# Splitting the first expert's weights on ScalarE and VectorE, with more list and expert steps for each attention tile

## The chip, the cores and the metric

The kernel runs on one core of a Trainium2 chip. The metric is the device time of the core in microseconds (us). Three runs of the kernel before took 971.29, 972.48 and 968.57 us; the median is 971.29 us. TensorE (PE) does the matmuls, VectorE (DVE) and ScalarE (ACT) the elementwise work, GpSimd (POOL) some elementwise work and the indirect DMAs, and SyncE (SP) issues most of the plain DMAs. Each engine works through its own list of instructions in order.

## The reference

Linear attention without a mask feeds a mixture of experts in which each token goes to two of eight experts:

```python
kv  = einsum('bhsd,bhse->bhde', k, v)            # 8 x 8 heads, 576 tokens, 64
out = einsum('bhsd,bhde->bhse', q, kv)
x   = out / sqrt(mean(out*out, -1) + 1e-6) * g_norm      # to [4608, 512]
noisy = x @ w_gate + log1p(exp(x @ w_noise)) * noise     # 8 experts
top2, weights = the two largest, softmax over them
y[t] = sum over the two experts e of weight * relu(x[t] @ w1[e]) @ w2[e]   # w1 512x1024, w2 1024x512
```

All is float32. The kernel gets near float32 accuracy in the experts by splitting each operand into two float16 parts, a high and a low one, and adding three float16 products.

## The kernel before, in words

**Attention stage.** The 4608 tokens are 36 tiles of 128 (t0 to t35); each of the 8 batches has four and a half of them. The loop at the end of the function goes over batches b and, in each, over its five pieces of tiles: every batch has one half tile, so tiles 4, 13, 22 and 31 come in two calls. A call of `tile_mm` (L590) multiplies a piece of q with the batch's `kvw`, into the PSUM tile `big`, of which there are two. `keep_warm` (L124) then adds matmuls of zeros, the fillers: KW = 8 a call while t < KT, KV2 = 0 from there. `steps` is `prep(b + 1)`, which makes the next batch's `kvw`: products of k and v (L558), a copy on ScalarE (L563), a transpose (L568), a copy `kvT` (L571), the gate products (L577) and a last copy into `kvw` (L580). `advance(t)` evacuates a tile on ScalarE (L598), squares and sums a pair of tiles (`sq` on ScalarE L605, `ss` on VectorE L607), makes the norm (`Ln` and `Exp` on ScalarE L611 and L612, three small VectorE operations), scales the pair on GpSimd (`lg` L621, `x` L625) and writes it out to `xs` in DRAM. A tile's matmul waits for the evacuation of the tile two before it.

**Lists.** `side` holds generators that make the expert lists, one for each chunk of tiles; the chunks end at tiles 10, 18, 28 and 36. `pump()` takes one step of each. A yield's number is how many pumps go by before the next step. `gating` finds the top two experts and counts places with matmuls into `RM` (L176, L178); `onehots` builds three tables on VectorE (`oa` L304, `ot` L307, `ob` L310); PY pumps later `place` (L318) multiplies them on PE. GY is the wait before the counting matmuls. For expert 0, `moe_early` then finishes the list, gathers the rows and, as soon as expert 0's weights are loaded, transposes them (`xpose`, L385 to L389) and queues `l1` (L434) and `l2` (L478) for two tiles, a unit, in `early`. `fill_early` takes one step of that queue. Three units of expert 0 are such early ones.

**First weights.** `w0 = first_weights()` is the generator `weights(0, wts_a, G, SL)`, of which the loop takes two steps a tile. It loads w1 of expert 0, takes column maxima on VectorE (`mx`, L221), shares them by a matmul with `dg` (L228, L232), and splits w1 in four slices of 128x1024; then the same for w2, whose load goes into the same buffer `rw`. In `split`, with `lo is G`, ScalarE scales a slice in place (L250), casts it to the float16 high part (L251), and GpSimd subtracts the two (L248). All later experts take the other branch: ScalarE scales and casts in one operation (L255), VectorE makes the low part in one operation (L257, L259).

**After the attention stage** the early units' remaining steps are taken from `early` (with list steps of expert 1, `locate`, between them: `oa`, `ot`, `ob` on VectorE and `place`), and then the loop over all other units runs. Its first unit in which the PE program branches on a count (`tc.Switch` in `l1`, L460 and L434) is the last unit of expert 0, here called the first switch.

All instructions stand in the order in which the code is written (`manual_schedule`), so these generators set the order on every engine.

## Time and profile before

| | |
|---|---|
| runs | 971.29, 972.48, 968.57 us |
| the profiled execution | 977.14 us, its span 975.3 us |
| mean granted TensorE clock | 0.965 |
| PE busy | 916.5 us (94%) |
| VectorE, ScalarE, GpSimd busy | 445.7, 327.5, 387.5 us |
| DMA | 143.33 MB, mean 147 GB/s |
| first attention tile's matmuls, last one's | start 19.2 us, start 153.3 us |
| first switch on PE | 234.0 us |

The profile is of one execution, whose own time is 5.9 us over the median of the runs. A page of it gives busy time by engine; the view of windows gives it for stretches of time together with the granted clock; the timeline lists instructions in order with the idle time before each and what released it.

### The profile page before, as it was taken

The page shows a single profiled execution, that of the slowest core. Times are in us where ns is not written, and L with a number is a line of the kernel's source. Part 1 is how long each engine was busy: PE and PEld are TensorE (multiplying, and loading weights), DVE is VectorE, ACT ScalarE, POOL GpSimd, SP SyncE. Part 2 cuts the span into 40 slices and gives each one's busy share as a digit, 9 for nine tenths or more (in the row PEclk, how much of TensorE's full clock was granted, in tenths as well). Part 3 has the DMA queues.
Part 4 walks back from the last instruction along what each step waited for, and adds up shares of the span by engine and source line. Part 5 has one row for each costly group of instructions (what it writes and reads, how often), then busy time and mean ns, then how long its engine had stood idle before and what let it go on. Part 6 is the DMA issues. An engine that isn't in the chain of part 4 may idle for free. (4 is left out here: it accounts for less than half of the span.)

```text
span 975.3 us, 15946 instructions
## 1 busy us (share of the span) xinstructions
PE 916.5 (94%) x6484; PEld 517.2 (53%) x6484; DVE 445.7 (46%) x936; ACT 327.5 (34%) x519; POOL 387.5 (40%) x412
## 2 busy tenths in 40 slices
PE   9976888988999999999999999999998989999995
PEld 8866775657444644464445444554443434644452
DVE  1648658554745543545353444455264447311110
ACT  1576543222522341233224332333243223332111
POOL 0456645153523542344245234414342544242122
PEclk9978799988999999999999999999999999999998
DMA  8999655952963864485357544666349735362224
GB/s 329 364 348 350 207 195 198 385 98 57 254 116 76 169 169 60 97 171 135 84 102 132 152 116 92 142 104 164 66 120 127 187 76 92 50 113 45 44 37 58
DMA packets 123534, 143.33 MB, mean 147 GB/s; under 512 B 79632, under 2 KB 79760, under 8 KB 123408
## 3 DMA queue, kind: packets, MB, share of 16 engines
q1 hardware_dynamic: 95696, 80.68, 30.2%
q0 software_dynamic: 17920, 41.95, 23.2%
q10 hardware_dynamic: 9792, 18.88, 5.1%
q8 instruction: 97, 1.59, 0.7%
q14 instruction: 29, 0.24, 0.1%
HBM read 83.02 MB, written 40.11 MB: 126 GB/s over the span
## 5 line engine op out<-in xcount | busy, mean ns | idle before, releaser
L434 PE MATMUL pp<-xT,w1h 128*128 128x512 f16 (+5 forms) x1600 | 367.8, 327 | 5.9 <-DVE oa L304 2.6
L478 PE MATMUL pp<-w2h,hT 128*128 128x512 f16 x1200 | 365.6, 381 | 5.4 <-ACT hT L439 4.1
L478 PEld LDWEIGHTS <-hT 128*128 128x128 f16 x1800 | 175.9, 98 | 214.0 <-issue 9.3
L412 POOL DMA_INDIRECT out_rows<-y,row x80 | 129.9, 1624 | 359.2 <-ACT y L503 354.5
L440 DVE SCALAR_TENSOR_TENSOR hT<-pp,hT 128x512 f16<-128x512 f32 x160 | 108.0, 688 | 353.7 <-ACT hT L439 353.6
L434 PE MATMUL pp<-xT,w1l 128*128 128x512 f16 (+5 forms) x800 | 256.8, 327 | 0.0
L478 PE MATMUL pp<-w2l,hT 128*128 128x512 f16 x600 | 228.2, 380 | 0.0
L434 PEld LDWEIGHTS <-w1h 128*128 128x128 f16 x1600 | 151.2, 100 | 112.2 <-issue 8.0
L439 ACT ACTIVATE hT<-pp 128x512 f16<-128x512 f32 x160 | 92.5, 596 | 265.7 <-PE pp L434 255.1
L503 ACT ACTIVATE y<-pp,gate 128x512 f32<-128x512 f32 x80 | 54.0, 686 | 258.6 <-PE pp L478 201.5
L360 POOL DMA_INDIRECT xg<-xs,idx x80 | 85.0, 1063 | 91.7 <-DVE la L332 43.5
L434 PEld LDWEIGHTS <-w1l 128*128 128x128 f16 x800 | 79.8, 100 | 56.5 <-issue 1.8
L368 POOL TENSOR_TENSOR xh<-xg,xh 128x512 f16<-128x512 f32 x70 | 91.4, 1380 | 35.7 <-ACT xh L367 35.6
L221 DVE TENSOR_REDUCE mx<-rw 128x1 f32<-128x1024 f32 x64 | 74.7, 1208 | 1.3 <-DMA rw<-w 1.3
L367 ACT ACTIVATE xh<-xg 128x512 f16<-128x512 f32 x70 | 41.1, 624 | 22.7 <-DMA xg<-xs,idx 18.8
L590 PE MATMUL big<-kvw,qt 64*128 64x80 f32 (+1 forms) x640 | 45.5, 287 | 2.2 <-ACT kvw L580 2.1
L304 DVE TENSOR_TENSOR oa<-jb,lnb 128x1152 bf16<-128x1152 bf16 (+2 forms) x32 | 46.3, 1448 | 0.0
L590 PEld LDWEIGHTS big<-kvw,qt 64*128 64x128 f32 (+1 forms) x640 | 39.1, 189 | 8.2 <-ACT kvw L580 2.8
L607 DVE TENSOR_REDUCE ss<-sq 128x16 f32<-128x1024 f32 x18 | 21.9, 1215 | 47.2 <-ACT sq L605 47.1
L411 POOL MEMSET tick<- 1x1 f32 x80 | 38.7, 484 | 0.0
L625 POOL TENSOR_TENSOR x<-o,ss 128x512 f32<-128x512 f32 x36 | 38.0, 1076 | 0.0
L257 DVE SCALAR_TENSOR_TENSOR w1l<-rw,sc,w1h 128x1024 f16<-128x1024 f32 x21 | 27.3, 1333 | 22.3 <-ACT w1h L255 22.3
(140 smaller groups left out, 587.7 us busy)
## 6 DMA issues: line engine op xcount, KB each, us to landing
rw<-w SPq DMA_DIRECT2D x64, 512.0 KB, 7.2
kvc<-kvm SPq DMA_DIRECT2D x32, 512.0 KB, 8.0
xs<-x ACTq DMA_DIRECT2D x18, 512.0 KB, 5.9
out_rows<-zrow ACTq DMA_DIRECT2D x18, 512.0 KB, 7.5
qt<-qt SPq DMA_DIRECT2D x8, 640.0 KB, 8.3
qt<-qt SPq DMA_DIRECT2D x8, 512.0 KB, 7.9
kvr<-kvr SPq DMA_DIRECT2D x4, 512.0 KB, 6.9
xg<-xs,idx POOLq DMA_INDIRECT x80, 3.9
```

Of the source, the lines that this page charges most:

```text
L221: V.tensor_reduce(mx[:, c:c + 1], src[:, c], axis=AX.X, op=OP.max, apply_absolute_value=True)
L304: V.tensor_tensor(oa, jb[:, None, :].to_broadcast([P, n, P]), lnb[:, s, e:e + 1].to_broadcast([P, n, P]), OP.is_equal)
L360: G.indirect_dma_start(out=x, out_offset=None, in_=src, in_offset=bass.IndirectOffsetOnAxis(ap=LI[e][:, t:t + 1], axis=0))
L367: A.activation(x[:, 0], XG[u, t], AF.Copy)
L368: G.tensor_tensor(x[:, 1], XG[u, t], x[:, 0], OP.subtract)
L412: d = G.indirect_dma_start(out=out, out_offset=bass.IndirectOffsetOnAxis(ap=LS[e][:, t:t + 1], axis=0), in_=y, in_offset=None, compute_op= ...
L434: T.matmul(ps[:, f % ps.shape[1], 0:n], w[wn][:, c, f * P:(f + 1) * P], x[:, xo + c, 0:n], start=(c == 0 and k == 0), stop=(c == HP - 1 an ...
L439: A.activation(h[:, 0, f:f + nf, 0:n], ps, AF.Relu)
L440: V.scalar_tensor_tensor(h[:, 1, f:f + nf, 0:n], ps, 0.0, h[:, 0, f:f + nf, 0:n], op0=OP.max, op1=OP.subtract)
L478: T.matmul(ps, h[:, hk, f, i * P:(i + 1) * P], w[wn][:, f], start=(f == 0 and k == 0), stop=(f == 7 and k == 2))
L503: A.activation(y, ps, AF.Copy, scale=LG[e][:, t:t + 1])
L590: T.matmul(TL[t][r0:r0 + n, h, hp * 80:(hp + 1) * 80], q[r, hp, s0 - o:s0 - o + n], KVW[b][r, hp], start=True, stop=True, skip_group_check ...
```

## The change

It has four parts.

1. The branch of `split` for GpSimd is gone. The first weights are split as all others: one ScalarE operation and one VectorE operation a slice. With the slack that only the first weights have, `split` yields after the ScalarE operation as well, so it takes ten steps where there were five; the up to three yields behind the first split are gone.
2. While t < EP = 24 the loop pumps the lists two more times a tile, so five times. GY goes from 3 to 5 and PY from 6 to 7.
3. `fill_early` is also called behind every call of `tile_mm`, so the early expert work advances by two steps a tile.
4. Fillers end at tile 14 where they ended at tile 24: 11 calls of 8 are gone, 88 matmuls of zeros.

```diff
-KT, KV2 = 24, 0
-XW, PY = 2, 6
+KT, KV2, EP = 14, 0, 24
+XW, PY = 2, 7
-GY = 3
+GY = 5
-    def weights(e, pool, lo, slack=0):
+    def weights(e, pool, slack=0):
-        def split(src, hi, lw, s):
-            if lo is G:
-                for c in range(5):
-                    if c:
-                        G.tensor_tensor(lw[:, c - 1], src[:, c - 1], hi[:, c - 1], OP.subtract)
-                    if c < 4:
-                        A.activation(src[:, c], src[:, c], AF.Copy, scale=s)
-                        A.activation(hi[:, c], src[:, c], AF.Copy)
-                    yield
-                return
+        def split(src, hi, lw, s, slack=0):
             for c in range(4):
                 A.activation(hi[:, c], src[:, c], AF.Copy, scale=s)
+                if slack:
+                    yield
                 if c:
-                    lo.scalar_tensor_tensor(lw[:, c - 1], src[:, c - 1], s, hi[:, c - 1], op0=OP.mult, op1=OP.subtract)
+                    V.scalar_tensor_tensor(lw[:, c - 1], src[:, c - 1], s, hi[:, c - 1], op0=OP.mult, op1=OP.subtract)
                 yield
-            lo.scalar_tensor_tensor(lw[:, 3], src[:, 3], s, hi[:, 3], op0=OP.mult, op1=OP.subtract)
+            V.scalar_tensor_tensor(lw[:, 3], src[:, 3], s, hi[:, 3], op0=OP.mult, op1=OP.subtract)
             yield
             yield
-        yield from split(r1, w["w1h"], w["w1l"], sc[:, 1:2])
-        for _ in range(min(slack, 3)):
-            yield
+        yield from split(r1, w["w1h"], w["w1l"], sc[:, 1:2], slack)
-        yield from split(r2, w["w2h"], w["w2l"], sc[:, 4:5])
+        yield from split(r2, w["w2h"], w["w2l"], sc[:, 4:5], slack)
         def first_weights():
-            yield from weights(0, wts_a, G, SL)
+            yield from weights(0, wts_a, SL)
...
                 tile_mm(*args)
+                fill_early()
                 keep_warm(KW if t < KT else KV2)
...
                 fill_early()
                 pump()
+                if t < EP:
+                    pump()
+                    pump()
...
-        yield from weights(e, wts_b if e % 2 else wts_a, V)
+        yield from weights(e, wts_b if e % 2 else wts_a)
```

What this moves is seen in the order of the instructions. First ScalarE behind the evacuation of tile 9 (`o<-big`), before; `rw<-rw,sc` and `w1h<-rw` are the two passes of the split, `kvw<-kvt` the copy that the next batch's transpose on PE needs:

```order
L598 ACTIVATE o<-big 128x640
L605 ACTIVATE sq<-o 128x1024
L250 ACTIVATE rw<-rw,sc 128x1024
L251 ACTIVATE w1h<-rw 128x1024
L250 ACTIVATE rw<-rw,sc 128x1024
L251 ACTIVATE w1h<-rw 128x1024
L563 ACTIVATE kvw<-kvt 128x4x64
L611 ACTIVATE ss<-ss,eps 128x16
L612 ACTIVATE ss<-ss 128x16
```

The same place now; the lines of the change's file are lower by 4 to 9:

```order
L589 ACTIVATE o<-big 128x640
L596 ACTIVATE sq<-o 128x1024
L246 ACTIVATE w1h<-rw,sc 128x1024
L554 ACTIVATE kvw<-kvt 128x4x64
L602 ACTIVATE ss<-ss,eps 128x16
L603 ACTIVATE ss<-ss 128x16
L589 ACTIVATE o<-big 128x640
L246 ACTIVATE w1h<-rw,sc 128x1024
```

Four passes of 128x1024 stood between `sq` and `kvw`; now it is one, and the next one stands behind the evacuation of tile 10.

Second, VectorE where the first chunk's tables are made, before (`vals` is the last step of the gating):

```order
L196 CAST vals<-gt_w 128x80
L304 TENSOR_TENSOR oa<-jb,lnb 128x1280
L307 TENSOR_TENSOR ot<-tb_101,t_115 128x100
L607 TENSOR_REDUCE ss<-sq 128x16
L310 TENSOR_TENSOR ob<-ot,vals 128x500
L630 TENSOR_REDUCE zl<-lg 128x32
```

And now:

```order
L196 CAST vals<-gt_w 128x80
L598 TENSOR_REDUCE ss<-sq 128x16
L295 TENSOR_TENSOR oa<-jb,lnb 128x1280
L221 TENSOR_REDUCE mx<-rw 128x1 x2
L298 TENSOR_TENSOR ot<-tb_101,t_115 128x100
L301 TENSOR_TENSOR ob<-ot,vals 128x500
L621 TENSOR_REDUCE zl<-lg 128x32
```

Two of w2's column maxima, which stood ahead of the gating's end, now stand between `oa` and `ob`. On PE the `place` that needs `ob` has moved from behind tile 19 to behind tile 17.

Third, VectorE just ahead of the first switch, before (`hT` is the low part of a unit's hidden layer):

```order
L440 SCALAR_TENSOR_TENSOR hT<-pp,hT 128x2x256
L307 TENSOR_TENSOR ot<-tb_101,t_115 128x90
L310 TENSOR_TENSOR ob<-ot,vals 128x450
L440 SCALAR_TENSOR_TENSOR hT<-pp,hT 128x2x256
L304 TENSOR_TENSOR oa<-jb,lnb 128x1152
L307 TENSOR_TENSOR ot<-tb_101,t_115 128x90
L310 TENSOR_TENSOR ob<-ot,vals 128x450
```

And now:

```order
L431 SCALAR_TENSOR_TENSOR hT<-pp,hT 128x2x256 x2
L295 TENSOR_TENSOR oa<-jb,lnb 128x1152
L298 TENSOR_TENSOR ot<-tb_101,t_115 128x90
L301 TENSOR_TENSOR ob<-ot,vals 128x450
L295 TENSOR_TENSOR oa<-jb,lnb 128x1152
L298 TENSOR_TENSOR ot<-tb_101,t_115 128x90
L301 TENSOR_TENSOR ob<-ot,vals 128x450
```

Behind the last `hT` there are two rounds of tables for expert 1's list where there was one; the `place` on PE that ends this stretch needs the last. From the first switch on PE's order is the same in both.

## The prediction

> **What bounds the kernel now.** I read the windows first: busy time by engine, then granted clock, DMA share and GB/s (columns PE, PEld, DVE, ACT, POOL).
>
> ```profile
> 44.00:51.70 7.70, 7.28 (x148) 6.35 (x146) 3.41 (x11) 5.40 (x8) 5.65 (x5) 1.00 0.89 328
> 51.70:68.00 16.30, 10.45 (x113) 8.70 (x114) 6.41 (x13) 12.61 (x21) 12.23 (x11) 0.59 0.89 328
> 68.00:88.90 20.90, 18.94 (x357) 17.04 (x354) 19.87 (x78) 8.42 (x18) 9.88 (x15) 0.99 0.96 371
> 88.90:109.00 20.10, 12.16 (x144) 10.37 (x144) 11.43 (x54) 14.81 (x24) 15.18 (x13) 0.58 0.63 221
> 109.00:155.00 46.00, 41.42 (x543) 33.12 (x543) 28.68 (x110) 23.81 (x48) 22.62 (x33) 0.96 0.56 190
> 155.00:234.00 79.00, 68.05 (x501) 47.54 (x500) 47.66 (x136) 21.50 (x35) 26.30 (x33) 0.92 0.67 207
> 310.00:950.00 640.00, 630.54 (x3459) 312.87 (x3457) 267.78 (x428) 198.33 (x297) 246.44 (x248) 0.99 0.54 109
> ```
>
> From 310 to 950 us PE is busy 630.54 of 640 us at full clock: nothing is to be had there, and the order is the same. What the change can move lies ahead of the first switch (234 us). There PE loses time in two ways. It stands idle: 5.85 us in 51.7 to 68, 7.94 in 88.9 to 109. And it runs slowly there: at 0.59, 10.45 busy us are 6.2 at full clock, a loss of 4.3; at 0.58, 12.16 lose 5.1. Those two windows lie on the two weight splits, and the view of waits for PE in 44 to 234 says on whom it waited (us, times, longest):
>
> ```profile
> PE kvt L568 <- ACT kvw L563: 5.9, 2, 3.9
> PE pp L385 <- DMA xg<-xs,idx: 5.9, 2, 3.6
> PE kvt L577 <- ACT kvT L571: 4.7, 2, 3.4
> PE M L318 <- DVE ob L310: 3.3, 1, 3.3
> ```
>
> The first and third are ScalarE's copies for the next batch, which queue behind the split. In the timeline, start and duration:
>
> ```profile
> 51.01 1.13 ACT L250 ACTIVATE rw<-rw,sc 128x1024 f32<-128x1024 f32 x1
> 52.18 1.06 ACT L251 ACTIVATE w1h<-rw 128x1024 f16<-128x1024 f32 x1
> ...
> 54.30 1.06 ACT L251 ACTIVATE w1h<-rw 128x1024 f16<-128x1024 f32 x1
> 55.27 0.36 ACT L563 ACTIVATE kvw<-kvt 128x256 f32<-128x256 f32 x1
> 55.69 1.06 PE L568 MATMUL kvt<-ident,kvw 128*64 128x128 f32 x4 [3.94 <-ACT kvw L563]
> ```
>
> Four passes from 51.01 on hold `kvw` to 55.27 and PE for 3.94 us; the clock then stays low to 68. So this stage is bound by a loop through PE, ScalarE and VectorE, each in order, and PE's clock punishes each wait. Between the splits, at 68 to 88.9, VectorE is the full engine: 19.87 of 20.9 us.
>
> **The change, part by part.** The new passes exist for expert 1 (mean ns behind the busy us; the VectorE row gives min/median/max), beside GpSimd's old one:
>
> ```profile
> L255 ACT ACTIVATE w1h<-rw,sc 128x1024 f16<-128x1024 f32 x8 | 8.9, 1136 | 0.0
> L257 DVE SCALAR_TENSOR_TENSOR w1l<-rw,sc,w1h x21: 1276/1283/2176, 193.2 to 817.4; 128x1024 f16<-128x1024 f32 x21
> L248 POOL TENSOR_TENSOR w1l<-rw,w1h x4: 2126/2127/2131, 49.5 to 58.9; 128x1024 f16<-128x1024 f32 x4
> ```
>
> For eight slices ScalarE gives up 8 x 1.06 = 8.5 us, GpSimd 8 x 2.13 = 17.0, and VectorE takes on 8 x 1.28 = 10.3. None of it is itself on PE; what counts is where PE's call of a tile lands. I line both kernels up by four calls: tiles 11, 14, 20, 23.
>
> ```profile
> 50.07 1.12 PE L590 MATMUL big<-kvw,qt 64*128 64x80 f32 x16
> ...
> 70.15 1.12 PE L590 MATMUL big<-kvw,qt 64*128 64x80 f32 x16
> ...
> 82.17 0.62 PE L124 MATMUL RM<-zrow 128*128 128x128 f16 x8
> 82.72 2.08 PE L558 MATMUL kvt<-kvc 128*64 128x64 f32 x64
> 84.74 0.68 PE L558 MATMUL kvt<-kvr 64*64 64x64 f32 x16
> 85.35 1.12 PE L590 MATMUL big<-kvw,qt 64*128 64x80 f32 x16
> ...
> 87.21 1.12 PE L590 MATMUL big<-kvw,qt 64*128 64x80 f32 x16
> ...
> 110.92 1.12 PE L590 MATMUL big<-kvw,qt 64*128 64x80 f32 x16
> ```
>
> From start to start, 8 fillers hold PE for 82.72 - 82.17 = 0.55 us and a batch's k-v products for 85.35 - 82.72 = 2.63.
>
> *Tiles 11 to 14* took 70.15 - 50.07 = 20.1 us, 5.8 of it idle and 4.3 low clock. `kvw` now stands behind one pass of 1.14 instead of four: its wait of 3.94 falls to about 0.5. The passes that went from ahead of it stand one each ahead of `kvT` and the batch's last copy; those copies also stand behind `Ln` and `Exp`, which wait for VectorE's `ss`. I put 1.8 us of wait at each. Idle is then 4.1 instead of 5.8, spread over three places, and I take the low clock as gone. Gain 1.7 + 4.3 = 6.0. Bounds: 1.7 if the clock falls all the same, 10.1 if no wait is left.
>
> *Tiles 14 to 20* took 17.1 us. Six calls' fillers go: 6 x 0.55 = 3.3 gained. Against it stands VectorE, whose rows here are
>
> ```profile
> 78.20 1.21 DVE L221 TENSOR_REDUCE mx<-rw 128x1 f32<-128x1024 f32 x1
> ...
> 82.35 1.48 DVE L304 TENSOR_TENSOR oa<-jb,lnb 128x1280 bf16<-128x1280 bf16 x1
> 83.75 0.40 DVE L307 TENSOR_TENSOR ot<-tb,t 128x100 bf16<-128x100 bf16 x1
> 84.07 1.21 DVE L607 TENSOR_REDUCE ss<-sq 128x16 f32<-128x1024 f32 x1
> 85.20 0.96 DVE L310 TENSOR_TENSOR ob<-ot,vals 128x500 bf16<-128x500 bf16 x1
> ```
>
> The `place` that needs `ob` now stands two tiles earlier on PE, and between `ss` and `ob` lie `oa` and two maxima of w2: from the end of tile 15's `sq` that is 1.2 + 1.5 + 2.4 + 0.4 + 1.0 = 6.5 us. PE has for this time two tile calls and the gate products, about 2.3 us: it waits some 4.2 us at `place`, and behind it are tile 18 and all else. The counting matmuls, a tile earlier too, wait about 1.7, and two more maxima ahead of tile 17's `ss` hold `Exp`, the evacuation behind it and tile 20 by about 1.4. So 7.3 us of new waits against 3.3: a loss of 4.0. Bounds: a gain of 3.3 if VectorE comes in time, a loss of 10 if the clock also falls to 0.58 over the stretch's 11.8 us of work (which would add up to 8.5, in part hidden under these waits).
>
> *Tiles 20 to 23* took 110.92 - 87.21 = 23.7 us: 7.9 idle, 5.1 low clock, four calls' fillers (2.2), the rest work. The second split's passes go one to a tile. I keep 2 us of wait at `kvT`. The batch's last copy now stands behind the second chunk's `Exp` for the gates, which waits for VectorE, and that for GpSimd's two gathers: I count 6.3 us of wait there, and 1.3 of low clock behind it. With two transposes (0.9) gone from here and 0.75 of counting matmuls come in, 23.7 becomes 17.4: gain 6.3. Bounds: 2.2 (fillers alone) to 13.
>
> *Tile 23 to the first switch.* Expert 0's second split ends later by tiles, so `l1` starts behind tile 28 instead of 24, but goes two steps a tile: by tile 35 its first unit's `l1` and `l2` are done, 30 matmuls further than before. The waits of this stretch I take as the same but for two:
>
> ```profile
> 170.44 0.97 PE L385 MATMUL pp<-ident,xg 128*128 128x128 f32 x4 [2.32 <-DMA xg<-xs,idx]
> ...
> 230.33 0.69 DVE L440 SCALAR_TENSOR_TENSOR hT<-pp,hT 128x512 f16<-128x512 f32 x1 [1.33 <-ACT hT L439]
> ...
> 232.48 0.63 DVE L310 TENSOR_TENSOR ob<-ot,vals 128x450 bf16<-128x450 bf16 x1
> 233.16 0.53 PE L318 MATMUL M<-ob,oa 128*128 128x50 bf16 x9 [3.27 <-DVE ob L310]
> ```
>
> The gathered rows of the third unit now have 96 matmuls ahead of their transpose where there were 60: the 2.32 us and some 1.5 of low clock behind it go, a gain of 3.8. Just ahead of the switch `ob` comes a round of tables later: between `hT`'s end (231.0) and `ob`'s (233.1) is 2.1 us, which PE waits in addition. Net gain 1.7; bounds -5 (every gather waits again) and +5.
>
> Sum: 6.0 - 4.0 + 6.3 + 1.7 = **10 us**. The profiled execution's span of 975.3 becomes 965.3; its own time, 977.14, lies 5.9 over the median of the runs, so from the median 971.3 I predict **961 us**.
>
> GpSimd loses 17 us of work that shared these stretches with VectorE, and this has a price of its own: a VectorE operation on two columns ended with the GpSimd pass beside it.
>
> ```profile
> 94.86 2.00 DVE L334 TENSOR_TENSOR row<-idx,la 128x2 int32<-128x2 int32 x1
> 94.72 2.13 POOL L248 TENSOR_TENSOR w2l<-rw,w2h 128x1024 f16<-128x1024 f32 x1 [1.95 <-ACT w2h L251]
> ```
>
> Both end at 96.86. The Trainium skill, "SBUF — State Buffer", section "SBUF: two separate sides", says that a VectorE operation with two SBUF inputs and a GpSimd operation that reads SBUF exclude each other for a whole instruction. The two rows agree. By this rule the new VectorE passes, which read `rw` and the high part, can each lose time to a GpSimd operation; the maximum of 2176 ns against a median of 1283 in the row above would be such a case. If half of eight lost 0.9, the second stretch would lose some 2 us more; I leave that inside its bounds.
>
> **The rivals.** *VectorE becomes the bound (chance 0.20).* The split, w2's maxima and the first chunk's tables fall on the engine that was 95% busy at 68 to 88.9. Then tiles 14 to 20 lose 10 and tiles 20 to 23 gain the fillers' 2.2 alone: 6.0 - 10 + 2.2 + 1.7 = 0, so 971. For it: the 19.87 of 20.9. Against: GpSimd's load is gone, and VectorE has gaps on both sides.
>
> *The clock stays low without fillers (chance 0.10, the slower side).* From tile 14 on PE has, by the windows, 18.9 + 7.1 + 39.8 = 65.6 us of work at full clock up to 155, less 6 of fillers: about 60, in the 86 us that I give it (tile 14 at 64, tile 35's end at about 150). At a clock of 0.58 that is 103: 17 more than the 86, so 10 - 17 = -7: 978. It decides from the point where the mean clock over this stretch falls under 60 / 96 = 0.63. For it: 0.59 and 0.58 where PE was busy for 64 and 60%, about the share that it will have from tile 14 to 23. Against: from tile 28 on `l1` fills PE, and at 90% busy the clock was 0.96.
>
> *Only long waits cost clock (chance 0.08).* A short wait did cost some:
>
> ```profile
> 133.00:140.00 7.00, 5.53 (x53) 4.32 (x51) 3.69 (x9) 3.53 (x10) 4.40 (x8) 0.76 0.47 170
> 135.87 0.63 PE L385 MATMUL pp<-ident,xg 128*128 128x128 f32 x4 [1.47 <-DVE ss L613]
> ```
>
> If this were rare, and a wait as short as the 1.7 and 2 us above left the clock at 1.0, the new stalls would overlap with work at full speed and the second stretch would lose 1 instead of 4: 958. The Trainium skill, "TensorE: Matmul & The Clock Gate", Part 1, says that the clock halves after an idle window of about 3.4 us. By that rule only the waits of 4.2 and 6.3 would cost; the row of 1.47 us speaks against it.
>
> **How the numbers follow.** My forecast has 0.62; it spans 954 to 967 by the terms' bounds, taken half way since not all go one way. Below 958 lies the third rival's side, above 967 the first and then the slower one. A range of 953 to 973 leaves out the slower rival and the far ends. A measurement tells a change of 0.5% (4.9 us) from none, so the marks are 966.4 and 976.2. Faster: nearly all of the forecast (0.58), the third rival (0.08) and a little of the first (0.04): 0.70. Same: 0.20. Slower: 0.10.
>
> **What would show it.** Tile 14's call near 64 us, tile 20's near 85, tile 23's near 102, the first switch near 224. ScalarE's `kvw` at once behind one pass; a wait of about 4 us on `ob` at the first `place`; a wait of 5 to 6 on the last `ob` ahead of the switch; the windows at 52 to 68 with a clock over 0.8. I am wrong if tile 14 comes after 67, if `place` waits over 8 us, or if the clock between 60 and 150 is under 0.63.

## The result: 16 us slower, and the profile after

The changed kernel takes 985.88 us (median of four runs, 985.13 to 987.70) against 969.93 us of the kernel before on the same chip: a ratio of 1.0164, 95% interval 1.0134 to 1.0195. The prediction was 961 us, with a range of 953 to 973, and faster. Its profiled execution took 987.7 us, its span is 985.9.

The kernel before varies by itself: runs made beside the experiments lay between 965 and 978 us, with medians of 971 to 973. Its first profiled execution, on which the prediction's stretches rest, took 977.14. It was therefore profiled again (run e18, below): 970.41 us, span 968.6. The shares below are read against both.

First the windows of the changed kernel, in the prediction's stretches: from the call of tile 11 to that of tile 14, 20, 23, to the end of the last tile, to the first switch, and the rest. The columns are the time, then busy time of PE, PEld, DVE, ACT and POOL, the granted clock, DMA share and GB/s.

```profile
52.20:67.10 14.90, 14.89 (x198) 13.09 (x198) 11.17 (x39) 8.29 (x15) 8.17 (x8) 0.58 0.94 368
67.10:90.20 23.10, 15.28 (x221) 13.85 (x219) 16.63 (x48) 8.52 (x18) 9.68 (x15) 0.70 0.90 325
90.20:107.90 17.70, 9.78 (x174) 8.74 (x173) 13.07 (x63) 10.17 (x19) 6.43 (x12) 0.71 0.75 270
107.90:160.20 52.30, 46.05 (x521) 35.60 (x519) 32.67 (x112) 25.00 (x48) 21.28 (x29) 0.93 0.44 164
160.20:243.40 83.20, 64.24 (x480) 44.67 (x479) 47.79 (x135) 20.46 (x34) 25.69 (x33) 0.93 0.65 197
243.40:985.90 742.50, 716.10 (x3951) 355.70 (x3951) 311.89 (x500) 225.39 (x340) 285.36 (x288) 0.99 0.54 111
```

The same stretches of the kernel before, in its second profile:

```profile
50.90:71.40 20.50, 15.34 (x198) 13.20 (x198) 10.18 (x25) 13.57 (x22) 13.12 (x12) 0.58 0.94 350
71.40:90.40 19.00, 18.00 (x272) 16.35 (x269) 16.64 (x65) 9.77 (x19) 11.22 (x15) 0.82 0.84 319
90.40:110.70 20.30, 14.41 (x207) 12.51 (x206) 12.21 (x55) 14.46 (x25) 15.03 (x17) 0.75 0.71 259
110.70:151.50 40.80, 37.24 (x504) 30.22 (x504) 27.22 (x104) 22.77 (x45) 20.95 (x28) 1.00 0.58 202
151.50:227.60 76.10, 64.36 (x505) 44.91 (x503) 48.38 (x141) 21.60 (x35) 26.69 (x35) 1.00 0.70 215
227.60:968.60 741.00, 714.70 (x3951) 355.61 (x3951) 311.93 (x501) 225.77 (x340) 285.72 (x288) 0.99 0.55 112
```

The first three stretches take 55.7 us against 59.8. The loss comes behind them: the fourth takes 11.5 us more (24 matmuls of `l2` moved into it, some 5 us, and its clock is 0.93 in place of 1.00) and the fifth 7.1 us more, although those 24 are gone from it. In the fifth PE has 480 matmuls in place of 505, and yet is idle for 83.2 - 64.24 = 19.0 us, against 76.1 - 64.36 = 11.7; and at a clock of 0.93 in place of 1.00 the 480 are busy for as long as the 505 were.

Seven of PE's waits up to the first switch, among them the five longest, in order of time (start, duration, what it is, in brackets the idle time ahead of it and what ended it):

```profile
52.21 2.00 PE L581 MATMUL big<-kvw,qt 64*128 64x80 f32 x16 [2.06 <-DMA qt<-qt]
81.65 0.57 PE L309 MATMUL RM<-ob,oa 128*128 128x50 bf16 x10 [6.56 <-DVE ob L301]
102.29 1.33 PE L581 MATMUL big<-kvw,qt 64*64 64x80 f32 x16 [6.19 <-ACT kvw L571]
184.35 1.08 PE L376 MATMUL pp<-ident,xg 128*128 128x128 f32 x4 [3.66 <-DMA xg<-xs,idx]
223.00 0.39 PE L425 MATMUL pp<-xT,w1h 128*128 128x256 f16 x1 [3.63 <-ACT xT L379]
240.44 0.39 PE L309 MATMUL M<-ob,oa 128*128 128x50 bf16 x9 [3.27 <-DVE ob L301]
242.53 0.53 PE L309 MATMUL M<-ob,oa 128*128 128x50 bf16 x9 [1.71 <-DVE ob L301]
```

The waits at 81.65 and 102.29 were forecast. Those behind 160 us hang on lists and gathers; how late those are is seen on VectorE and GpSimd. `m` is the copy of a list that has just been placed. Changed kernel, the third list and expert 0's last one, and the first gather behind the latter:

```profile
174.73 0.20 DVE L318 COPY m<-RM 128x50 f32<-128x50 f32 x1
208.66 0.20 DVE L318 COPY m<-RM 128x50 f32<-128x50 f32 x1
210.17 0.99 POOL L351 DMA_INDIRECT xg<-xs,idx  x1 [14.35 <-DVE m L326]
```

Before (second profile):

```profile
161.04 0.20 DVE L327 COPY m<-RM 128x50 f32<-128x50 f32 x1
193.80 0.20 DVE L327 COPY m<-RM 128x50 f32<-128x50 f32 x1
195.31 0.99 POOL L360 DMA_INDIRECT xg<-xs,idx  x1 [12.51 <-DVE m L335]
```

The last list is ready 14.9 us later, the switch comes 15.8 us later. Counted from the end of the last tile the list comes after 48.5 us in place of 42.3.

### The profile page after: what moved, and what is told of

Its sections match the earlier page's. It is cut to its first block, busy times and chain, and to the rows that moved or that the text cites. A ratio compares the mean times of both kernels' runs of the same rounds, so it can differ in the third digit from the quotient of the medians.

```text
span 985.9 us, 15761 instructions
## 1 busy us (share of the span) xinstructions
PE 913.1 (93%) x6396; PEld 514.0 (52%) x6396; DVE 453.3 (46%) x944; ACT 319.1 (32%) x511; POOL 368.1 (37%) x404
## 5 line engine op out<-in xcount | busy, mean ns | idle before, releaser
L469 PEld LDWEIGHTS <-hT 128*128 128x128 f16 x1800 | 175.7, 98 | 215.9 <-issue 11.5
L221 DVE TENSOR_REDUCE mx<-rw 128x1 f32<-128x1024 f32 x64 | 74.6, 1208 | 2.7 <-DMA rw<-w 2.6
L581 PE MATMUL big<-kvw,qt 64*128 64x80 f32 (+1 forms) x640 | 48.5, 298 | 8.3 <-ACT kvw L571 6.2
L581 PEld LDWEIGHTS big<-kvw,qt 64*128 64x128 f32 (+1 forms) x640 | 41.9, 200 | 14.7 <-ACT kvw L571 6.6
L250 DVE SCALAR_TENSOR_TENSOR w1l<-rw,sc,w1h 128x1024 f16<-128x1024 f32 x24 | 31.1, 1326 | 22.3 <-ACT w1h L246 22.3
L250 DVE SCALAR_TENSOR_TENSOR w2l<-rw,sc,w2h 128x1024 f16<-128x1024 f32 x24 | 29.8, 1284 | 15.5 <-ACT w2h L246 15.5
```

What stands on the lines that cost most here:

```text
L221: V.tensor_reduce(mx[:, c:c + 1], src[:, c], axis=AX.X, op=OP.max, apply_absolute_value=True)
L250: V.scalar_tensor_tensor(lw[:, c - 1], src[:, c - 1], s, hi[:, c - 1], op0=OP.mult, op1=OP.subtract)
L469: T.matmul(ps, h[:, hk, f, i * P:(i + 1) * P], w[wn][:, f], start=(f == 0 and k == 0), stop=(f == 7 and k == 2))
L581: T.matmul(TL[t][r0:r0 + n, h, hp * 80:(hp + 1) * 80], q[r, hp, s0 - o:s0 - o + n], KVW[b][r, hp], start=True, stop=True, skip_group_check ...
```

## The experiments

Four theories were put against each other at first. A: the second early step of a tile uses up matmuls that later cover the list, gather and scatter chains. B: the additional yields of the split make everything behind it late. C: the additional list steps move `place` and the gates ahead of VectorE. D: the missing fillers cost clock. Later ones were G (the constants GY and PY) and H (the chain behind the last tile). All ratios are to the kernel before on the same chip, with 95% intervals; they reach 2 to 6 us to either side, so a cost given as a difference of two medians is uncertain by 3 us or more.

### One part undone (e1 to e3), one part alone (e4)

e1 takes out the second early step:

```diff
                 tile_mm(*args)
-                fill_early()
```

> The changed kernel without the second early step of a tile (the call of fill_early behind tile_mm is gone; split, pumps, table constants and filler end stay). Theory A (the doubled early steps use up the matmuls that later cover the list, gather and scatter chains, and bring ScalarE to the wait for a y buffer, 13.58 us at 221.28 of the changed kernel): the stretch from the end of the last tile to the first switch loses about 10 us of its waits, the y wait falls back to about 4.5 us as before, and the time comes to 971 to 977 us. Theory B (the split's additional yields make the first weights, the w2 load and the first early unit late, and this is what costs): nothing in the split changes here, so the time stays at 983 to 988 us. Theory C (the two additional pumps move place and gate work ahead of VectorE): also 983 to 988. Theory D (the missing fillers cost clock): also 983 to 990, since even less work of use stands between the tiles.

e2 takes out the list steps with their constants:

```diff
-XW, PY = 2, 7
+XW, PY = 2, 6
-GY = 5
+GY = 3
-                if t < EP:
-                    pump()
-                    pump()
```

> The changed kernel without the two additional list steps a tile, and with the list constants GY and PY back at 3 and 6; split, second early step and filler end stay. Theory C (the pumped list steps bring place and the gates to VectorE early, with the 6.56 us wait of place at 81.65 and the 6.19 us wait for the last kvw copy at 102.29): tile 23 is called some 8 us earlier than in the changed kernel and the time comes to 976 to 980 us. Theory A (early steps): the lists end later, the early units too, and the time stays at 983 us or rises to 990, because the cover is used up as early and the lists are later still. Theory B (yields of the split): 983 to 988. Theory D (clock): 983 to 988.

e3 keeps the fillers to tile 24 (`KT = 24`):

> The changed kernel with the fillers kept up to tile 24 as before (KT = 24), all else as changed. Theory D (the granted clock of 0.58 to 0.71 between 52 and 108 us is low because the fillers are gone, and this costs): the granted clock of that window comes back to 0.85 or more and the time to 973 to 979 us. Theories A, B and C: the clock rises, but the fillers themselves cost about 88 times 38 ns = 3.3 us at the most and the waits for VectorE, ScalarE and lists stay, so the time is 982 to 990 us.

e4 is the kernel before with part 1 of the change alone, the new `split`:

> The kernel before with the new split alone: the first weights are split in one pass each of ScalarE and VectorE with ten yields for each matrix, as in the changed kernel; one early step a tile, the list steps and the fillers as before. Theory B (the split's ten yields make the first early unit late: its l1 begins behind tile 28 in place of tile 24): the time rises to 976 to 984 us. Theories A, C and D: the split takes four ScalarE scale passes and four GpSimd passes a matrix away and lays its work where PE does not wait for it, so the time is 966 to 972 us, that of the kernel before or a little below.

Measured: e1 981.59 us (1.0112, 1.0059 to 1.0165), e2 976.05 (1.0041, 1.0014 to 1.0067), e3 983.85 (1.0121, 1.0092 to 1.0150), e4 963.14 (0.9917, 0.9883 to 0.9951).

B falls: the split alone makes the kernel faster by 8 us. D is at most a small part: in e3 the mean clock from 52 to 108 us rose from 0.67 to 0.77, and the time fell by 2.0 us only, which is not clear of the noise. (That is net of the fillers themselves, which are dearer than the expectation has it: by the prediction's 0.55 us for eight, 88 hold PE for some 6 us.) The list steps with their constants cost most (9.9 us), the second early step 4.3, less than A said, though ScalarE's wait for a `y` buffer fell from 13.58 to 4.53 us, as A expected. No two of these add up to the loss of 16 us, so each part was next added to the split by itself.

### One part added to the split (e5 to e7)

Each starts from e4 and adds the lines shown above for e1, for e2, and `KT = 14`.

> The kernel with the split alone (963.1 us) and the second early step of a tile added. Each part costs what it does by itself (sum theory): the changed kernel lost 4.3 us by the second step (985.9 less 981.6), so 965 to 969 us here. Order theory (the second step is harmful only where the pumps have moved the lists, or harmful by itself because the fifth y then stands ahead of the xT copies of the fourth unit): if it is harmful by itself, ScalarE shows the wait of some 13.6 us for a y buffer here too and the time is 967 to 973; if it is harmful only with the pumps, no such wait and 961 to 965.

> The kernel with the split alone (963.1 us) and the two additional list steps a tile with GY = 5 and PY = 7 added. Sum theory: the changed kernel lost 9.9 us by the pumps (985.9 less 976.05), so 971 to 975 us here, with a wait of place for VectorE of 5 us or more and one for the last kvw copy of 4 us or more between 75 and 105 us. Rival (the pumps only cost in company with the second early step, whose matmuls they displace): 961 to 967 us.

> The kernel with the split alone (963.1 us) and the fillers ended at tile 14. Sum theory: the changed kernel lost 2.0 us by the missing fillers (985.9 less 983.85), so 963 to 967 us. Clock theory (without fillers the clock falls in every wait of 75 to 105 us, which the other parts hid): the granted clock of 75 to 100 us falls from 0.73 to below 0.66 and the time is 967 to 973 us. If the waits leave room for more matmuls of use: 959 to 963 us.

Measured: e5 971.77 us (1.0012, 0.9984 to 1.0041), e6 976.87 (1.0055, 1.0028 to 1.0083), e7 966.09 (0.9929, 0.9900 to 0.9957). From 963.1 that is 8.6, 13.7 and 3.0 us; the sum, 25.3, is near the 22.7 that lie between e4 and the changed kernel. e5 and e6 lie 2 to 3 us above what the sum theory gave them, so the second early step harms by itself (its wait for a `y` buffer is there too, 13.71 us), and so do the list steps; the 3.0 us of e7 are within the noise. In e7 the clock of 75 to 100 us fell to 0.60, as the clock theory said, but the time rose by no more than the sum theory's 4 us.

The windows up to the end of the last tile, to the first switch and to the end show how. e4:

```profile
0.00:146.10 146.10, 123.59 (x2001) 109.17 (x2002) 91.84 (x305) 71.48 (x135) 60.34 (x83) 0.89 0.82 303
146.10:221.40 75.30, 70.66 (x533) 48.68 (x533) 47.59 (x138) 20.92 (x35) 26.40 (x35) 0.98 0.71 217
221.40:962.30 740.90, 715.96 (x3951) 355.07 (x3951) 315.34 (x503) 226.73 (x342) 285.43 (x288) 0.99 0.54 112
```

e5, with the second early step:

```profile
0.00:157.20 157.20, 136.59 (x2055) 116.98 (x2056) 93.89 (x314) 72.76 (x137) 60.75 (x84) 0.90 0.76 282
157.20:233.80 76.60, 63.84 (x480) 44.93 (x479) 46.01 (x130) 20.45 (x34) 26.43 (x33) 0.93 0.69 213
```

e5 does 54 matmuls more ahead of the last tile's end, and 53 fewer behind it; the last tile ends 11.1 us later, and the stretch behind it is 76.6 us as against 75.3. PE's idle time there grows from 4.6 to 12.8 us. So the work that the second step brings forward costs its time in front and saves none behind: the stretch lasts about 75 us either way. (The part behind the switch took 736.3 us in this profile, 4.6 less than in e4, which gives some of it back; that was not followed up.)

### Constants or list steps (e9, e10)

`GY` and `PY` count list steps that a chunk of tiles waits. The additional steps are given only up to tile 24. Behind the last tile the loop is

```
    while side:
        pump()
        fill_early()
```

so there a chunk gets one list step for each step of `l1` or `l2`, and larger constants hold the last two chunks back by whole steps of expert work. e9 has the constants without the steps, e10 the steps without the constants:

> The kernel with the split alone (963.1 us), with GY = 5 and PY = 7 in place of 3 and 6 and no additional list step. Theory G (the larger constants are steps that the last two chunks, of tiles 18 to 27 and 28 to 35, must also wait, where a tile or an early step gives only two or three list steps; so the last lists, gathers and scatters come later and the stretch from the end of the last tile to the first switch grows from 75 to 85 us as with the pumps): that stretch is 83 to 87 us and the time 971 to 977 us. Theory C (the additional list steps themselves cost, by their waits on VectorE and ScalarE between 75 and 105 us): the stretch stays at 74 to 78 us and the time at 961 to 967.

> The kernel with the split alone (963.1 us), with the two additional list steps a tile up to tile 24, and GY = 3, PY = 6 as before. Theory G (the constants cost): the stretch behind the last tile is 74 to 78 us, and the time 961 to 967 us. Theory C (the additional steps cost): place and kvw waits of 4 us or more each, the last tile ends 4 us or more later than at 146.1 us, and the time is 968 to 976 us.

Measured: e9 972.23 us (1.0024, 0.9994 to 1.0054), e10 966.57 (0.9954, 0.9931 to 0.9977): 9.1 us for the constants and 3.4, at the edge of the noise, for the steps. e9's stretch behind the last tile:

```profile
147.80:233.20 85.40, 73.14 (x535) 49.61 (x533) 50.79 (x147) 22.08 (x36) 26.14 (x35) 0.96 0.62 191
```

It has e4's work and takes 85.4 us, as G said; e10's takes 76.1. In e9 the last list of expert 0 is copied at 194.94, in e4 at

```profile
185.00 0.20 DVE L318 COPY m<-RM 128x50 f32<-128x50 f32 x1
186.51 0.99 POOL L351 DMA_INDIRECT xg<-xs,idx  x1 [11.01 <-DMA out_rows<-zrow]
```

Of the waits that C expected, one is there in e10 (4.68 us for the last `kvw` copy at 96.89; `place` waits 1.60 us only), but the last tile ends at 148.0 us, only 1.9 later.

### Is the stretch bound by the chain? (e11)

e11 is e5 without the third of the three `l2` passes of the early units, so their output lacks that part of the product. (There are three early units, not four as the expectation has it; the 48 matmuls are theirs.)

```diff
-        passes = ((0, "w2h"), (0, "w2l"), (1, "w2h"))
+        passes = ((0, "w2h"), (0, "w2l"), (1, "w2h"))[0:2 if u < EARLY else 3]
```

> The kernel with the split and the second early step (971.8 us), with the third of the three l2 passes left out for the four early units: 48 matmuls of about 0.22 us, 10.4 us of TensorE work, of which 14 (3 us) stand ahead of the end of the last tile and 34 (7.4 us) behind it. The output lacks that part of the product. Theory H (the stretch behind the last tile is set by the chain of gate, place, list and gather, not by TensorE's work): only the 3 us ahead of the tile end and at most 2 us behind it are gained, 966 to 970 us, and the idle time of that stretch grows from 12.8 to 17 us or more. Rival (TensorE's work sets it): 10 us are gained, 959 to 963 us.

Measured: 972.80 us (1.0009, 0.9984 to 1.0035), against 971.77 of e5. 10.4 us of matmuls less gain nothing.

```profile
0.00:152.20 152.20, 133.70 (x2041) 115.54 (x2042) 93.89 (x304) 72.74 (x137) 60.74 (x83) 0.89 0.78 291
152.20:229.30 77.10, 57.60 (x446) 41.83 (x447) 48.50 (x141) 20.47 (x34) 27.32 (x33) 0.90 0.69 212
229.30:974.20 744.90, 718.94 (x3951) 357.50 (x3951) 312.77 (x501) 225.26 (x340) 286.95 (x288) 0.98 0.54 111
```

The stretch behind the last tile is 77.1 us long with 57.60 busy, where e5 has 76.6 with 63.84: H's first half holds. The 3 us expected in front were gained in this profile (the last tile ends 5.0 us earlier), but the part behind the switch took 744.9 us against 736.3. Its matmuls are the same 3951, and 6.3 of the 8.6 us are their busy time (718.94 against 712.62); why the clock was lower there was not followed up. The profiled execution, 976.04 us, is 3.2 over its median. The medians show nothing gained, and the time lies above H's 966 to 970 us too: what the runs show is that the stretch does not get shorter, not where the 3 us in front went.

### What the split gains (e12)

e12 takes the additional yields out of `split`, and keeps its one pass an engine:

> The kernel with the split alone (963.1 us) without the additional yields between a ScalarE pass and its VectorE pass: six yields a matrix in place of ten (before: seven and five). If the gain of 8 us over the kernel before comes from the work that the split leaves out (four ScalarE passes and four GpSimd passes a matrix), the time is 961 to 966 us here. If it comes from the later start of the first early unit (its l1 behind tile 28 in place of tile 24), which keeps 11 l1 and 18 l2 matmuls as cover behind the last tile, the time is 967 to 972 us and the first l1 stands behind tile 24 or 25 again.

Measured: 966.43 us (0.9952, 0.9922 to 0.9981). Its last tile ends at 149.8, with 503 matmuls behind it, and the switch comes 76.1 us later; in e4 it ends at 146.1, with 533 behind it, and the switch comes 75.3 us later. So the longer split's part in the gain, some 3 us, goes the way of e5 backwards: 30 matmuls less ahead of the last tile's end, and no time more behind it. The intervals of e4 and e12 overlap, so this 3 us is read from the traces and not shown by the times. Its first `l1` stands behind tile 24 again, as in the kernel before, and yet it is 4.5 us faster than that kernel: this rest is put down to the leaner passes. The measured time lies at the seam of the two expectations, and both parts are in the gain.

### The constants in the changed kernel, and earlier lists (e13 to e16)

e13 is the changed kernel with `GY = 3`, `PY = 6`. e14 is the split with `GY = 2`, `PY = 4`; e15 the split with one more list step a tile from tile 24 on and in the four steps behind the last; e16 is e15 with `GY = 2`, `PY = 5`.

> The changed kernel with GY = 3 and PY = 6 as before; split, additional list steps, second early step and filler end stay. Theory G (the constants hold back the last two lists by one to one and a half list steps of a tile each): the stretch from the end of the last tile to the first switch falls from 83.3 to 73 to 77 us and the time to 975 to 979 us. Rival (with the second early step no matmuls are left to cover the lists wherever they stand): the stretch stays above 80 us and the time at 983 to 988.

> The kernel with the split alone (963.1 us) with GY = 2 and PY = 4 in place of 3 and 6. Theory H (the chain of gate, place, list and gather sets the stretch behind the last tile, 75.3 us with 4.6 us idle): the lists come earlier, but no more than the 4.6 us of idle time can be gained there, and place may wait for VectorE in the tiles: 959 to 966 us. Rival (VectorE is not done by then, and TensorE waits at the earlier places and gates): the waits for VectorE behind 140 us grow to 3 us or more each, and 966 to 974 us.

> The kernel with the split alone (963.1 us) with one more list step a tile from tile 24 on, and in the four steps behind the last tile; constants as before. Theory H: the last two lists come some 12 to 24 matmuls earlier, the gather waits of 2.43 and 0.92 us shrink, and the time is 959 to 963 us. Rival (waits for VectorE take their place): 963 to 970 us.

> The kernel of the run before with GY = 2 and PY = 5 besides. Theory H: 957 to 963 us, with less than 4 us idle between the end of the last tile and the first switch. Rival (TensorE reaches place before VectorE has the one-hot products): waits of 3 us or more for VectorE at the last two places of the first list, and 965 to 973 us.

Measured: e13 979.45 us (1.0085, 1.0053 to 1.0117), with 74.6 us behind the last tile: the constants cost 6.4 us in the changed kernel, the largest single part there as well, and the stretch is as short as G said. e14 982.20 (1.0106, 1.0044 to 1.0167), e15 980.20 (1.0087, 1.0057 to 1.0117), e16 986.85 (1.0161, 1.0097 to 1.0224): all three are slower than e4 by 17 to 24 us, and above the ranges of their rivals too. They do not tell what earlier lists would gain, because the last list, which that stretch hangs on, did not come earlier: it is copied at 195.60, 194.27 and 194.55 us, where e4 has it at 185.00. So this half of H, that the 4.6 us which stood idle in e4 can be gained, stays open. e14's rows show waits of the kind that its rival named; e4's first, then e14's, with its last list and the time up to the end of the last tile:

```profile
119.50 0.36 PE L309 MATMUL RM<-ob,oa 128*128 128x50 bf16 x8 [1.93 <-DVE ob L301]
151.56 0.41 PE L309 MATMUL RM<-ob,oa 128*128 128x50 bf16 x10 [1.46 <-DVE ob L301]
```

```profile
122.56 0.49 PE L309 MATMUL RM<-ob,oa 128*128 128x50 bf16 x8 [5.64 <-DVE ob L301]
162.20 0.41 PE L309 MATMUL RM<-ob,oa 128*128 128x50 bf16 x10 [2.56 <-DVE ob L301]
195.60 0.21 DVE L318 COPY m<-RM 128x50 f32<-128x50 f32 x1 [1.74 <-PE RM L309]
0.00:158.20 158.20, 132.69 (x2001) 117.15 (x2002) 94.20 (x310) 72.40 (x135) 61.67 (x84) 0.84 0.77 283
```

PE reaches `place` before VectorE is done; behind 140 us the waits for it are under the 3 us that the rival put (2.56 us here). Up to the end of the last tile, 12.1 us later than in e4, PE is idle only 3.0 us longer (25.5 against 22.5); the other 9.1 us are the same 2001 matmuls running slower, at a clock of 0.84 in place of 0.89. e14 also loses 4.0 us between the last tile and the switch (79.3 against 75.3) and 7.9 behind it (748.8 against 740.9), which was not followed up; its profiled execution, 988.12 us, is 5.9 over its median. So the old constants stand at a narrow place: a few steps more make the chain longer (e9), a few steps fewer cost waits and clock and bring the last list no sooner.

### The scatters and the y buffer (e8, e17)

In the changed kernel ScalarE waits long for one of the four `y` buffers, which the scatters free:

```profile
221.28 0.69 ACT L494 ACTIVATE y<-pp,gate 128x512 f32<-128x512 f32 x1 [13.58 <-DMA out_rows<-y,row]
```

That looked like the cause of the 3.63 us that PE waits for `xT` at 223.00. e8 puts the scatters ahead of a gather in `moe_early`, and with them all zero fills that are still due. It stands ahead of the third and last early unit's gathers, not of those at 210 us, as the expectation has it:

```diff
+        if u == EARLY - 1:
+            while clear():
+                pass
+            scatter()
         gather(u)
```

> The changed kernel with the scatters of the first y tiles, and the zero fills they wait for, put on their queues ahead of the gathers of the fourth early unit. Theory A in its narrow form (the 13.58 us wait of ScalarE for a y buffer is what costs, since the scatters stand on GpSimd behind the gathers at 210 us): the wait falls below 3 us, PE's wait of 3.63 us for xT at 223 us goes, and the time is 980 to 983 us. Rival (the list of the fourth unit, with the gathers at 210 us, is late anyway and its xT copies cannot come earlier): the time stays at 984 to 988 us.

Measured: 1010.03 us (1.0366, 1.0319 to 1.0412). The 14 fills of 512 KB in one piece hold ScalarE's issue from 174.81 for 18.97 us:

```profile
174.81 18.97 ACTq L393 DMA_DIRECT2D out_rows<-zrow  x14
193.82 0.22 ACT L154 ACTIVATE gt_d<-gt_d 128x8 f32<-128x8 f32 x1 [18.42 <-DMA out_rows<-zrow]
194.58 0.61 PE L469 MATMUL pp<-w2h,hT 128*128 128x512 f16 x1 [13.31 <-ACT hT L430]
210.93 1.09 PE L376 MATMUL pp<-ident,xg 128*128 128x128 f32 x4 [13.62 <-DMA xg<-xs,idx]
```

So it answered another question. e17 moves the scatters alone, ahead of the gathers at 210 us:

```diff
+    while clear():
+        pass
+    scatter()
     finish(0, M0, slice(2 * EARLY, CAP))
     gather(EARLY)
```

> The changed kernel (985.9 us) with the first four scatters on GpSimd directly ahead of the gathers at 210 us in place of directly behind them; no zero fill moves. If the wait for the y buffer is what costs: the scatters run in the idle time of GpSimd between 196 and 210 us, ScalarE's wait of 13.58 us falls below 3 us, TensorE's wait of 3.63 us for xT at 223.00 goes, and the time is 980 to 983 us. If the gathers and their list (read from the place of the last chunk at 204.83 us) set this point anyway: the y wait falls and the time stays at 984 to 988 us.

Measured: 986.62 us (1.0147, 1.0102 to 1.0191), that is, unchanged. ScalarE's wait fell from 13.58 to 2.72 us and PE's wait for `xT` went; in its place PE waits for the gather:

```profile
210.42 1.56 POOL L403 DMA_INDIRECT out_rows<-y,row  x1 [0.27 <-ACT y L494]
212.29 1.58 POOL L351 DMA_INDIRECT xg<-xs,idx  x1 [0.30 <-issue]
216.86 1.12 PE L376 MATMUL pp<-ident,xg 128*128 128x128 f32 x4 [5.94 <-DMA xg<-xs,idx]
```

But the gathers were held up as well: the scatters ran from 204.42 us on, and the first gather stands behind the fourth of them, 4.4 us behind its list (copied at 207.90), where in the changed kernel it comes 1.5 us behind (208.66 to 210.17). So one wait was traded for another. That the wait for the `y` buffer costs nothing, and that the last list alone sets this point, is not shown.

### The kernel before once more (e18)

> The kernel before, unchanged. Its median is 970 to 973 us. If its first profiled execution was typical in its stretches, the last tile ends at 152 to 156 us, the first switch comes at 231 to 236 us with some 11 us idle between, and the rest takes 735 to 742 us; if the 6 us by which it stood above the median lie ahead of the switch, the switch comes at 226 to 230 us.

Measured: 972.13 us against 972.62 beside it (0.9997, 0.9970 to 1.0024). Its switch comes at 227.6 us in place of 234.0, and the rest takes 741.0 us as before (741.3): all of the 6 us by which the first profiled execution stood above the median lay ahead of the switch.

## Why the prediction was wrong

By its own steps, in us gained (+) or lost (-):

| stretch | predicted | against the first profile | against the second |
|---|---|---|---|
| up to tile 11 | 0 | -2.1 | -1.3 |
| tiles 11 to 14 | +6.0 | +5.2 | +5.6 |
| tiles 14 to 20 | -4.0 | -6.1 | -4.2 |
| tiles 20 to 23 | +6.3 | +6.0 | +2.6 |
| tile 23 to the first switch | +1.7 | -12.4 | -18.5 |
| from there | 0 | -1.2 | -1.5 |
| sum | +10.0 | -10.6 | -17.3 |

**The step that failed is the term of tile 23 to the first switch**, +1.7 us put and -12.4 or -18.5 measured, and in it the sentence that the waits of this stretch are the same but for two. It took the matmuls that the second early step brings forward as progress ("30 matmuls further than before"). They make tile 23 to the end of the last tile longer (52.3 us where the two profiles before have 43.5 and 40.8) and what is behind no shorter: the stretch behind the last tile is set by the chain of gates, `place`, list and gather, so that work taken out of it shortens nothing (e5, e11). And it left out that GY and PY hold also for the chunks that get no additional list steps; the part of them that lies behind tile 24 was not costed at all (e9: 9.1 us, e13: 6.4 us). Its bound of -5 ("every gather waits again") allowed for waits at the same places, not for a longer chain. The two waits that it did name: the third unit's gather wait of 2.32 us did not go but became 3.66 us at 184.35, and the round of tables ahead of the switch came, with two waits of 3.27 and 1.71 us, 5.0 together, where one of 5 to 6 was put.

Of the prediction's own signs, tile 14's call came at 67.08 us (64 put, "wrong if after 67"), tile 20's at 90.21 (85), tile 23's at 107.94 (102) and the switch at 243.4 (224).

**Tiles 11 to 14: right sum, in this profile by luck.** `kvw` comes at once behind one pass, and the wait of 3.94 us is gone. But the other waits that were forecast at `kvT` and the last copy did not come, and the low clock, which was taken as gone, stayed: PE is busy for 14.89 of 14.90 us at 0.58. The idle time of 5.8 us went whole, the clock did not, and the two errors cancel. Another execution shows the forecast itself: in e17, whose instructions are the same up to there, the load of `qt` makes PE wait 0.32 us ahead of tile 11 in place of 2.06, tile 14 is called at 64.78, the waits at `kvT` and the last copy are there (1.11 and 2.04 us, 1.8 put for each), and the clock is 0.88:

```profile
50.70:64.80 14.10, 10.90 (x198) 9.75 (x198) 12.00 (x38) 9.44 (x19) 8.17 (x8) 0.88 1.03 405
```

Both take about the same time, 14.9 and 14.1 us: at the low clock PE works through the time in which it else waits for the copies.

**Tiles 14 to 20: right in kind, not in the cause.** `place` waits for `ob` behind two maxima of w2, 6.56 us where 4.2 was put. The difference is on VectorE: `oa` took 2.32 us where 1.5 was put, and the maxima themselves wait 1.74 us for w2:

```profile
78.08 2.56 DVE L221 TENSOR_REDUCE mx<-rw 128x1 f32<-128x1024 f32 x2 [1.74 <-DMA rw<-w]
```

The load of w2 is issued at 67.18 us; before, that was at 61.02. The split's yields moved the load, and no term stood for that. Nor is it the list steps that bring the wait here: in e2, which has none of the additional ones, `place` waits 9.37 us for `ob`, and with the split alone (e4) VectorE waits 6.12 us for w2, and PE 7.66 us for VectorE behind it:

```profile
76.71 1.22 DVE L221 TENSOR_REDUCE mx<-rw 128x1 f32<-128x1024 f32 x1 [6.12 <-DMA rw<-w]
80.51 1.01 PE L124 MATMUL RM<-zrow 128*128 128x128 f16 x8 [7.66 <-DVE gap L188]
```

In e4 the load is issued at 65.94 us. In e12, without the additional yields, it is issued at 57.73 and VectorE waits 1.03 us for it. So even the fastest version stands still here for a load that comes late.

**Tiles 20 to 23: right in place and size** against the profile it was made from: 6.19 us of wait for the last `kvw` copy where 6.3 was put, 1.72 at `kvT` where 2 was put. In the second profile of the kernel before this stretch takes 20.3 us in place of 23.7, so 3.4 us of the gain were that first execution's own. As written the prediction's sum for this stretch comes to about 18.0 us and not 17.4; it comes out with the low clock of the whole stretch (15.75 us busy at 0.64, a loss of 5.7) in place of 5.1.

**The rivals.** That VectorE becomes the bound did not come about: that case had tiles 14 to 20 lose 10 and tiles 20 to 23 gain 2.2. The slower rival had the sign right and the cause wrong: the mean clock from 60 to 150 us is 0.80, above its 0.63, and fillers to tile 24 give back 2.0 us of the 17 it put on them. That only long waits cost clock is refuted by the row of 52.20 to 67.10: a clock of 0.58 behind a wait of 2.06 us. The rule of the Trainium skill, "TensorE: Matmul & The Clock Gate", Part 1, that the clock halves after an idle window of about 3.4 us, is not borne out here either, as the row of 1.47 us had suggested.

The eight new VectorE passes took 1.27 to 1.37 us each in the changed kernel, so the 2 us that the prediction left inside its bounds for them did not come. Where two of them started ahead of GpSimd's `lg`, it was `lg` that took longer (1.50 and 1.53 us, 0.62 else); where GpSimd's `x` had started ahead of VectorE's `oa`, `oa` did (2.32 us, 1.48 before). That agrees with the rule of the Trainium skill, "SBUF — State Buffer", section "SBUF: two separate sides", by which one of the two excludes the other for a whole instruction.

**What the whole is made of.** Added to the split alone (963.1 us): constants 9.1, second early step 8.6, additional list steps 3.4, fillers to 14 3.0, together 24.1; measured 22.7. The last two are each no larger than the noise. The first part of the change, 8 us faster by itself, is by its median the fastest version of all that ran; the three others cost nearly three times that.

## What to carry to other kernels

Where a stretch is set by a chain of small steps on several engines, work moved out of it is lost twice: it takes time where it is put, and the chain is left without cover; compare idle time and length of that stretch, not the count of matmuls done. A count in program steps (wait so many steps) must be costed at every place where the steps have another length, above all at the end, where one list step is a whole step of expert work. Taking away a long wait must be costed by what the remedy itself holds up: when the y wait of 13.58 us was taken away by earlier scatters, these held the gathers, a wait of 5.94 us took its place, and the time stayed. And fewer program steps ahead of a list need not bring it sooner: in e14 to e16 the last list came 9 to 11 us later.

## What the runs showed of the hardware that was not expected

**A short wait can hold the clock at half for 10 us of full work.** Changed kernel, windows behind the wait for `qt` of 2.06 us that ends at 52.21:

```profile
50.00:52.20 2.20, 0.14 (x3) 0.03 (x1) 1.90 (x4) 2.17 (x6) 0.00 (x0) 0.77 0.97 291
52.20:55.50 3.30, 3.29 (x27) 3.08 (x28) 1.53 (x3) 2.60 (x4) 2.77 (x3) 0.50 1.03 407
55.50:58.90 3.40, 3.40 (x29) 2.67 (x27) 2.83 (x4) 3.17 (x6) 0.74 (x1) 0.50 1.03 416
58.90:62.30 3.40, 3.40 (x47) 3.03 (x48) 3.25 (x8) 0.65 (x3) 1.92 (x2) 0.50 1.03 421
62.30:65.70 3.40, 3.40 (x66) 3.03 (x64) 2.16 (x13) 1.88 (x3) 2.75 (x4) 0.63 0.76 296
65.70:69.00 3.30, 2.81 (x65) 2.57 (x60) 3.16 (x28) 1.50 (x4) 0.00 (x0) 1.00 0.87 300
```

PE has work for 10.09 of the 10.10 us from 52.20 to 62.30 and is granted 0.50. The Trainium skill, "TensorE: Matmul & The Clock Gate", Part 1, says that the clock returns after about 3.4 us of sustained work and falls after an idle window of about 3.4 us; here 2.06 us of waiting were enough to lose it, and it took at least 10 us to come back. It need not take that long: in e17 a wait of 2.04 us up to 59.40 was followed by 0.51 from 60.5 to 64.0 only, and by 1.00 from there, which agrees with 3.4 us for the way back. Busy time is the profile's model of PE's work, but the clock is the granted one. The same may be how 3.0 us of additional idle time became 12.1 us in e14; that was not tried by itself.

**Zero fills issued in one piece block their engine.** 14 DMA issues of 512 KB took ScalarE's queue 18.97 us (e8), and two waits of over 13 us on PE followed; spread over the steps, as in the changed kernel, the longest row of them (three issues) took 4.20 us, and no wait up to the switch is put down to them.
